# Decay attention and mixer: a new SBUF layout on the right side, pair-wise masks and token sums, operand builds and stores at other places

## The chip, the core and the metric

One NeuronCore of one Trainium2 chip runs the whole kernel. The metric is device time in microseconds (us). Three runs of the kernel before took 592.5, 596.78 and 596.5 us, median 596.5.

## The reference, cut to what matters

```python
# q, k, v: [B=4, H=8, S=768, D=64]; lam: [8], one decay per head
for b in range(nb):                       # blocks of 64 positions
    intra = einsum('bhic,bhjc->bhij', qb, kb) * Dmask     # lam ** (i - j), lower triangle
    intra = einsum('bhij,bhjd->bhid', intra, vb)
    inter = einsum('bhid,bhde->bhie', qb * lam_pow, kv_state)
    out[:, :, sl] = intra + inter
    kv_state = lam_block * kv_state + einsum('bhsd,bhse->bhde', kb * rev_pow, vb)
x = out.transpose(0, 2, 1, 3).reshape(B, S, 512)
# mixer: w_tok1 [768, 256], w_tok2 [256, 768], w_ch1 [512, 1536], w_ch2 [1536, 512], all float64
u = x + transpose(relu(transpose(x) @ w_tok1) @ w_tok2)
return u + relu(u @ w_ch1) @ w_ch2        # float32, [4, 768, 512]
```

The reference's blocks have 64 positions; the kernel computes the same recurrence in chunks of 128.

## The kernel before, in words

**Layout.** `uT[b]` holds the attention's output of batch b, and later the mixer's u, turned: 128 feature rows, 4 feature tiles, 768 positions. Every product of the mixer is made from a high and a low float32r half of each factor and takes three matmuls (high with high, low with high, high with low).

**Order.** The order in which the code is written is the order of each engine's queue. There is no scheduler that moves anything; an instruction that waits holds up all that stands behind it on its engine.

**Attention.** A loop `i` from -2 to 15 goes over 16 pairs (a batch and two heads) and works on several of them at once. For pair i+1 it makes scores (PE) and multiplies them with the decay masks (DVE, L306), scales the queries (POOL, L250), and makes the state (PE, a scan on DVE, and a copy `stb` on POOL, L284). For pair i it makes the outputs (L321, L331), copies them to `uT` (ACT, L338) and turns them back to positions (`turn_back`: PE L353, ACT L361 for `xhi`, DVE L362 for `xlo`). Groups of the token mixer are taken into the same loop (`take`): `token_hidden` (12 or 18 matmuls into `ph`, L444, then ACT and DVE write `hh` and `hl`) and `token_out` (6 matmuls into `pu`, L464, then a DVE add into `uT`, L469). Side work stands in the deque `waiting`, and `later(n)` takes n steps of it at fixed points.

**Weights.** The float64 weights arrive as pairs of 32-bit words. `narrow` turns 512 columns into float32 in five steps: one on ACT (L379) and four on DVE (L380, L383, L386, L389). `split` writes the high half on ACT (L371) and the low half on POOL (L372). The channel weights come in six groups of four pieces each, 0 and 1 for `c1`, 2 and 3 for `c2`. Seven combinations of `c1`'s blocks (A11, A12, A22, S1 to S4) are needed, since a channel product is done as a two-by-two block product with seven instead of eight multiplications; `split_c1` makes them with four sums on DVE (L512 to L515) and four splits.

**Operands.** `build(b, n)` makes the other factors of batch b from `uT[b]`: B11, B21, B22 and T1 to T4, each as a high half (ACT, L560) and a low half (L562, on POOL, or on DVE where `on_vector` names it). The temporaries behind T1 to T4 are DVE differences t1 to t4 (L552, L568).

**Hand-over.** After the loop 12 token groups of the last batch are left; between them stand parts of `build(1, 1)`. Then `p1.close()` gives the right side of SBUF (token weights, `hh`, `hl`, `x` halves) back, and the pool `cp` takes it.

**Channel mixer.** 24 units follow: for b = 0, 1 the weight groups 0 to 5, then for b = 2, 3 the groups 5 to 0. A unit has seven products `m1` to `m7` of six matmuls (L717) and four `out_pair`s of twelve matmuls (L794), each followed by a DVE add into `uT` (L809). `SLOTS` says in which order they stand; `background(n)` says after how many matmuls of unit n which side work is issued. `m3` accumulates onto the PSUM bank of `m5`, so it waits until the sum `c22` (L768) has read it; `m7` does so with the bank of `m6` (L750). Groups are written to DRAM after narrowing (`save`) and read back for b = 2, 3 (`restore`). Four `hidden_parts` results go through ACT and POOL (L728 to L730).

**Stores.** In the last units of each half `out_pair` turns its result with DVE transposes (L818) into `y` and issues eight DMAs of 48 KB (L822). The last block goes through PE transposes into `ylast` and leaves in three DMAs (`finish`, L844).

Of the kernel before, what the change touches and what calls it, by code (L numbers as in the profile page):

```python
# [22 lines left out]
def kernel(  # L23
# [264 lines left out]
    def scores(i):  # L288
        b, p = pairs[i]
        for g in range(2):  # L290
            pair = two_banks(f"sc{i}{g}", 3 * P)
            sc = [pair[:, h] for h in range(2)]
            for c in range(3):
                cs = slice((3 * g + c) * P, (3 * g + c + 1) * P)
                for h in range(2):
# [7 lines left out]
                    )  # L303
            for h in range(2):
                a = ap.tile([P, 3, P], F32, tag="a", bufs=8, name=f"a{i}{g}{h}")
                nc.vector.tensor_mul(  # L306
                    out=a,
                    in0=sc[h].rearrange("p (c i) -> p c i", i=P),
                    in1=mask[:, 2 * p + h, None, :].broadcast_to([P, 3, P]),
                )  # L310
# [141 lines left out]


# [26 lines left out]
    A11, A12, A22, S2, S3, S4, S1 = range(NW)  # L480

    def group_tiles(n, pool):
        return (
            pool.tile([P, NW, 2, P], F32R, tag="c1h", name=f"c1h{n}"),
            pool.tile([P, NW, 2, P], F32R, tag="c1l", name=f"c1l{n}"),
            pool.tile([P, JG, DM], F32R, tag="c2h", name=f"c2h{n}"),
            pool.tile([P, JG, DM], F32R, tag="c2l", name=f"c2l{n}"),
        )
# [221 lines left out]
    def prod(nm, to, a, o, start):  # L710
        g, b = nm
        c1h, c1l, _, _ = weights[g]
        uh, ul = ops[b][o]
        i = 0
        for t in range(2):
            for w, x in ((c1h, uh), (c1l, uh), (c1h, ul)):
                nc.tensor.matmul(  # L717
                    out=to, lhsT=w[:, a, t], rhs=x[:, t], start=(start and i == 0), stop=(i == 5),
# [297 lines left out]
```

## Time and profile before

| | |
|---|---|
| runs | 592.5, 596.78, 596.5 us; median 596.5 |
| profiled execution | 596.63 us, its span 594.8 us |
| ACT | 214.5 us busy, 36% |
| POOL | 237.6 us busy, 40% |
| `out_pair` adds (L809) | 94, 89.6 us in all |
| masks (L306) | 64, 31.2 us in all |

The engines' times overlap, so their sum is larger than the span. Where PE is busy nearly all the time, another engine's time shows only where PE waits for it. The rows of a trace give the start and the length of an instruction, and in brackets the idle time before it with the instruction whose end freed it. The stretches that matter are the attention loop (about 10 to 180 us), the hand-over (about 183 to 223), the first half of the units to about 370, the second half, and the end from 565.

### The profile page before, as it was taken

Reading aid. Unit: us, or ns where it says so; the run is one execution under the profiler, and the core shown is the slowest. Engines: PE = TensorE matmul, PEld = TensorE weight load, DVE = VectorE, ACT = ScalarE, POOL = GpSimd, SP = SyncE. Lnnn points to the kernel's source line nnn. Section 1 sums busy time; section 2 is a strip of 40 time slices with the busy share of each in tenths; the row PEclk is TensorE's granted clock in tenths of the full one; section 3 lists DMA queues with packets and bytes.
Section 4 is the critical chain, followed back from the end, with each engine's and each line's share of the span. In section 5 each row is a group of like instructions: output and inputs, shape, how many; then the busy total and the mean of one; then the engine's idle time right before and its main releaser. Section 6 shows DMA issues by size and latency. Waiting matters only on the chain.

```text
span 594.8 us, 10627 instructions
## 1 busy us (share of the span) xinstructions
PE 562.8 (95%) x4234; PEld 542.0 (91%) x4234; DVE 407.8 (69%) x633; ACT 214.5 (36%) x426; POOL 237.6 (40%) x205
## 2 busy tenths in 40 slices
PE   5998999799998979999999997999999999999994
PEld 4888889699998879999999997999999999999993
DVE  4797886767768788878878898974444444444472
ACT  3564433324244444344444344442222222222220
POOL 6675632455217444435344364872112222222220
PEclk9998999889999999999999999999999999999998
DMA  9999998868000227272725300464313132320057
GB/s 187 257 241 181 176 213 168 152 122 155 1 2 1 72 71 266 71 266 72 259 79 207 130 0 1 67 89 60 123 72 125 71 125 72 123 72 1 0 81 132
DMA packets 174289, 67.80 MB, mean 114 GB/s; under 512 B 163360, under 2 KB 164512, under 8 KB 174240
## 3 DMA queue, kind: packets, MB, share of 16 engines
q1 hardware_dynamic: 170896, 66.05, 44.8%
q10 hardware_dynamic: 3344, 1.09, 0.8%
q8 instruction: 33, 0.54, 0.4%
q14 instruction: 16, 0.13, 0.1%
HBM read 49.29 MB, written 17.83 MB: 113 GB/s over the span
## 4 chain that ended last, share of the span: by engine, by line
PE 76%; DVE 11%; issue 4%; ACT 3%; DMA 2%; POOL 2%; SPq 0%; ACTq 0%; POOLq 0%
PE po L794 28%; PE pc L717 8%; PE pa L717 7%; PE pb L717 7%; PE ph L444 5%; PE xT L321 4%; PE pu L464 4%; PE sc L297 4%; PE pd L717 4%; PE xT L331 2%; DMA vn<-in_v_dram 1%; DVE uT L809 1%; DVE cs L552 1%; PE xp L353 1%; PE kv L263 1%
## 5 line engine op out<-in xcount | busy, mean ns | idle before, releaser
L809 DVE TENSOR_TENSOR uT<-po,uT 128x768 f32<-128x768 f32 x94 | 89.6, 954 | 67.2 <-PE po L794 67.0
L730 POOL TENSOR_TENSOR h22l<-c,h22h 128x384 fp32r<-128x384 f32 x24 | 25.8, 1075 | 155.1 <-ACT h22h L729 143.8
L728 ACT ACTIVATE c<-c 128x384 f32<-128x384 f32 x72 | 37.8, 525 | 123.3 <-DVE c L768 90.6
L284 POOL COPY stb<-sv 64x320 f32<-64x320 f32 x32 | 26.7, 833 | 53.0 <-DVE sv L271 47.6
L321 PE MATMUL xT<-a,vn 128*64 128x128 f32 x384 | 37.5, 288 | 1.3 <-ACT uT L338 1.0
L338 ACT COPY uT<-xT 128x384 f32<-128x384 f32 x32 | 15.3, 478 | 59.6 <-PE xT L331 57.1
L730 POOL TENSOR_TENSOR h12l<-c,h12h 128x384 fp32r<-128x384 f32 x24 | 24.8, 1033 | 29.4 <-PE pa L717 20.8
L306 DVE TENSOR_TENSOR a<-sc,mask 128x384 f32<-128x384 f32 x64 | 31.2, 548 | 6.7 <-PE sc L297 6.5
L750 DVE TENSOR_TENSOR u<-pb,s 128x384 f32<-128x384 f32 x24 | 13.4, 557 | 29.7 <-PE pb L717 19.1
L756 ACT ACTIVATE h11h<-pa 128x384 fp32r<-128x384 f32 x24 | 11.7, 487 | 61.1 <-PE pa L717 61.1
L372 POOL TENSOR_TENSOR c1l<-cs,c1h 128x512 fp32r<-128x512 f32 (+1 forms) x20 | 23.3, 1177 | 25.4 <-ACT c1h L371 25.4
L331 PE MATMUL xT<-qs,stb 128*64 128x128 f32 x320 | 32.0, 278 | 0.0
L444 PE MATMUL ph<-xhi,w1h 128*128 128x256 f32 x96 | 28.2, 294 | 0.8 <-DVE uT L469 0.5
L730 POOL TENSOR_TENSOR h21l<-c,h21h 128x384 fp32r<-128x384 f32 x24 | 26.4, 1099 | 4.5 <-ACT h21h L729 3.1
L321 PEld LDWEIGHTS xT<-a,vn 128*64 128x64 f32 x384 | 23.0, 141 | 5.6 <-ACT uT L338 2.3
L297 PE MATMUL sc<-qT,kT 64*128 64x128 f32 x384 | 27.6, 293 | 0.2 <-ACT qT L235 0.2
L297 PEld LDWEIGHTS sc<-qT,kT 64*128 64x128 f32 x384 | 24.4, 200 | 3.5 <-issue 1.9
L444 PE MATMUL ph<-xhi,w1l 128*128 128x256 f32 x96 | 27.1, 282 | 0.0
L444 PE MATMUL ph<-xlo,w1h 128*128 128x256 f32 x96 | 27.1, 282 | 0.0
L464 PE MATMUL pu<-w2h,hh 128*128 128x384 f32 x64 | 24.0, 374 | 3.1 <-DVE uT L469 2.1
L250 POOL TENSOR_TENSOR qs<-qT,lamp 128x640 f32<-128x640 f32 x16 | 25.3, 1583 | 0.3
L362 DVE TENSOR_TENSOR xlo<-xp,xhi 128x384 fp32r<-128x384 f32 x32 | 17.7, 553 | 10.1 <-ACT xhi L361 9.9
(261 smaller groups left out, 1897.6 us busy)
## 6 DMA issues: line engine op xcount, KB each, us to landing
raw<-in_moe_w_ch_dram SPq DMA_DIRECT2D x20, 512.0 KB, 3.7
vn<-in_v_dram SPq DMA_DIRECT2D x16, 384.0 KB, 5.0
kn<-in_k_dram SPq DMA_DIRECT2D x30, 192.0 KB, 4.6
out_dram<-y SPq DMA_DIRECT2D x110, 48.0 KB, 1.9
qn<-in_q_dram SPq DMA_DIRECT2D x44, 96.0 KB, 3.1
dw<-c1h SPq DMA_DIRECT2D x4, 896.0 KB, 6.1
dw<-c1l SPq DMA_DIRECT2D x4, 896.0 KB, 7.9
c1hr<-dw SPq DMA_DIRECT2D x4, 896.0 KB, 4.4
```

Of the source, the lines that this page charges most:

```text
L284: nc.gpsimd.tensor_copy(out=st[r, :, h, :], in_=sv[r].rearrange("p (e c) -> p c e", c=NC - 1))
L297: nc.tensor.matmul(out=sc[h][:, c * P : (c + 1) * P], lhsT=kTs[i][r, cs], rhs=qTs[i][r, cs], start=True, stop=True,)
L306: nc.vector.tensor_mul(out=a, in0=sc[h].rearrange("p (c i) -> p c i", i=P), in1=mask[:, 2 * p + h, None, :].broadcast_to([P, 3, P]),)
L321: nc.tensor.matmul(out=xT[h * D : (h + 1) * D, cs], lhsT=vns[i][:, h, c, :], rhs=weights_of[i, g, h][:, cg, :], start=(cg == 0), stop=False,)
L331: nc.tensor.matmul(out=xT[h * D : (h + 1) * D, cs], lhsT=st[:, c - 1, h, :], rhs=qss[i][:, c - 1, :], start=False, stop=(cg == 2),)
L444: nc.tensor.matmul(out=ph, lhsT=w[:, c, fs], rhs=x[:, c], start=(i == 0), stop=(i == 3 * NC - 1))
L464: nc.tensor.matmul(out=pu, lhsT=h[:, kk, cs], rhs=w[:, kk, ss], start=(i == 0), stop=(i == 3 * NK - 1))
L717: nc.tensor.matmul(out=to, lhsT=w[:, a, t], rhs=x[:, t], start=(start and i == 0), stop=(i == 5), skip_group_check=not start,)
L728: nc.scalar.activation(src, src, AF.Relu)
L730: nc.gpsimd.tensor_sub(out=hl, in0=src, in1=hh.bitcast(F32))
L794: nc.tensor.matmul(out=to, lhsT=w[:, jj, t * P : (t + 1) * P], rhs=h, start=(i == 0), stop=(i == 3 * JG - 1))
L809: nc.vector.tensor_add(out=ub, in0=po, in1=ub)
```

## The change

- A new pool `hidp` on the right side outlives the token phase. It holds `w2h`, `w2l`, `hh0`, `hl0`, `hh1` and `hl1`. After the token phase the odd weight groups' `c1` take `w2h` and `w2l`, their `c2` take `hh1` and `hl1`, and raw pieces and the stores' `y` take `hh0` and `hl0`. A11 has tiles of its own, so a group is saved and restored by six DMAs instead of four.
- One DVE instruction of 128 x 768 masks the scores of both heads: 32 instructions instead of 64.
- Group 0: the four sums of `split_c1` go from DVE to POOL at i = 7. The narrowing and the split of piece 2 are queued at i = 9 instead of 8, B11 and B21 of `build(0, 0)` at i = 10 instead of 9.
- The last eight `token_out`s become four `token_out_pair`s, 12 matmuls into two banks and one add of 128 x 768. Pieces 0 and 1 of group 1 are fetched ahead of them; steps of narrowing and of `build(1, 1)` stand between them. T1 of that build goes to POOL; t3, T3, t4 to unit 0; T4 and B22 to unit 1. The side work of units 0 and 1 is written out anew.
- Units 10 to 12: the builds for b = 2, 3 stand at other places, with T1 to T4 of both on DVE (before: T1 and T2 of one).
- The stores of b = 0, 1 (64 DMAs, 16 transposes) go from units 11 and 12 to units 13 to 20. The units (1, 2) and (0, 2) are done before (1, 3), (0, 3): the last three `(0,2), (1,3), (0,3)` instead of `(1,3), (0,2), (0,3)`. The stores of b = 2 are spread over the last two units.

```diff
+    hidp = ctx.enter_context(tc.tile_pool(name="hidp", bufs=1, side="right"))
     p1 = ExitStack()
...
+            a = ap.tile([P, 2, 3, P], F32, tag="a", bufs=4, name=f"a{i}{g}")
+            nc.vector.tensor_mul(
+                out=a,
+                in0=pair.rearrange("p h (c i) -> p h c i", i=P),
+                in1=mask[:, 2 * p : 2 * p + 2, None, :].broadcast_to([P, 2, 3, P]),
+            )
             for h in range(2):
-                a = ap.tile([P, 3, P], F32, tag="a", bufs=8, name=f"a{i}{g}{h}")
-                nc.vector.tensor_mul(
...
+    def token_out_pair(b, sh, ct):
...
+        pu = two_banks(f"pu{b}{ct}{sh}", SB)
...
+        u = uT[b][:, ct : ct + 2, ss]
+        nc.vector.tensor_add(out=u, in0=pu, in1=u)
...
+    def group_tiles(n, odd):
+        pools = (cp, cp, hidp, hidp, hidp, hidp) if odd else (wa,) * 6
+        tags = ("a11h", "a11l", "w2h", "w2l", "hh1", "hl1") if odd else NAMES
...
-            lambda: nc.vector.tensor_add(out=a22, in0=a21, in1=a22),
+            lambda: eng.tensor_add(out=a22, in0=a21, in1=a22),
...
-            waiting.extend(split_c1(weights[0], w3[:, 0:512], w3[:, 512:1024]))
+            waiting.extend(split_c1(weights[0], w3[:, 0:512], w3[:, 512:1024], nc.gpsimd))
             load_piece(0, 3, w3[:, 2048:3072])
-        if i == 8:
+        if i == 9:
             waiting.extend(narrow_piece(w3[:, 1024:2048], w3[:, 0:512], w3[:, 512:1024]))
             waiting.append(split_c2(weights[0], 2, w3[:, 0:512]))
-        if i == 9:
+        if i == 10:
...
-    parts = build(1, 1, on_vector=("T2", "T1"))
-    order = deque(parts[x] for x in ("B11", "t1", "t2", "B21", "T2", "T1", "t3", "T3"))
-    while groups:
+    for _ in range(4):
         groups.popleft()()
...
+    fetch(1, 0)
+    fetch(1, 1)
+    steps = {}
+    parts = build(1, 1, on_vector=("T2",))
+    pa, pb = piece_steps(0), piece_steps(1)
+    order = [
+        [parts["t1"], parts["B11"], pa[0], pa[1]],
+        [parts["t2"], pa[2], parts["B21"], pa[3]],
+        [parts["T2"], pa[4], lambda: fetch(1, 2)],
+        [parts["T1"]],
+    ]
+    for n, fs in enumerate(order):
+        token_out_pair(B - 1, n // 2, 2 * (n % 2))
+        for f in fs:
+            f()
...
+    units[-3], units[-2] = units[-2], units[-3]
...
+        if n == 0:
+            c1, pb = steps["c1"], piece_steps(1)
+            add(12, pb[0], pb[1], pb[2], c1[0])
+            add(36, parts["t3"])
+            add(36, parts["T3"])
+            add(36, pb[3], pb[4], lambda: fetch(1, 3))
+            add(42, c1[1], parts["t4"])
+        if n == 1:
+            c1, pa = steps["c1"], piece_steps(2)
+            add(6, parts["T4"])
+            add(24, c1[2], c1[3], c1[4], c1[5], c1[6], pa[0])
+            add(36, parts["B22"])
+            add(36, pa[1], pa[2], c1[7])
+            add(60, pa[3], pa[4], lambda: fetch(2, 0))
...
-            bl = build(2, 0, cs_temps(), on_vector=("T2", "T1"))
+            second["a"] = bl = build(2, 0, cs_temps(), on_vector=("T1", "T2", "T3", "T4"))
...
-            bl = build(3, 1, cs_temps())
+            second["b"] = bl = build(3, 1, cs_temps(), on_vector=("T1", "T2", "T3", "T4"))
...
+        if NP1 + 1 <= n < NP1 + 9:
+            x = n - NP1 - 1
+            add(36, lambda: store(x // 4, x % 4))
+        if n >= NU - 2:
+            x = 2 * (n - NU + 2)
+            add(36, lambda: store(2, x))
+            add(84, lambda: store(2, x + 1))
```

The next fences show queues: the line of code, the operation, output and inputs with a number for each tile, the shape, and a count where rows are alike. First POOL around i = 7 to 9, before; `uT_63` holds group 0's narrowed pieces, `qs` scaled queries, `stb` states.

```order
L284 COPY stb_116<-sv_1383 64x5x64 x2
L372 TENSOR_TENSOR c1l_1037<-uT_63,c1h_1036 128x256
L372 TENSOR_TENSOR c1l_1037<-uT_63,c1h_1036 128x512
L250 TENSOR_TENSOR qs_1514<-qT_1399,lamp 128x640
L284 COPY stb_114<-sv_1539 64x5x64 x2
L372 TENSOR_TENSOR c1l_1037<-uT_63,c1h_1036 128x512 x2
L372 TENSOR_TENSOR c2l_1039<-uT_63,c2h_1038 128x512
L250 TENSOR_TENSOR qs_1669<-qT_1555,lamp 128x640
```

The same place of POOL's queue now:

```order
L286 COPY stb_119<-sv_1348 64x5x64 x2
L375 TENSOR_TENSOR a11l_1012<-uT_63,a11h_1011 128x256
L375 TENSOR_TENSOR c1l_1014<-uT_63,c1h_1013 128x512
L534 TENSOR_TENSOR uT_63<-uT_63 128x2x128
L535 TENSOR_TENSOR uT_63<-uT_63 128x2x128
L536 TENSOR_TENSOR uT_63<-uT_63 128x2x128
L537 TENSOR_TENSOR uT_63<-uT_63 128x2x128
L252 TENSOR_TENSOR qs_1475<-qT_1364,lamp 128x640
L286 COPY stb_117<-sv_1500 64x5x64 x2
L375 TENSOR_TENSOR c1l_1014<-uT_63,c1h_1013 128x512 x2
L252 TENSOR_TENSOR qs_1619<-qT_1516,lamp 128x640
L286 COPY stb_119<-sv_1644 64x5x64 x2
```

The four sums (L534 to L537) stand ahead of the scaled queries, and the split of piece 2 (`c2l`) has gone one pair of heads further back.

DVE at the hand-over, before; `uT_63` is the last batch, `pu` the token sums, `th`, `tl` the temporaries of `build(1, 1)`, `u_0` and `s_0` belong to unit 0:

```order
L552 TENSOR_TENSOR th_2463<-uT_61 128x768
L469 TENSOR_TENSOR uT_63<-pu_2465,uT_63 128x384
L552 TENSOR_TENSOR tl_2473<-uT_61,th_2463 128x768
L469 TENSOR_TENSOR uT_63<-pu_2475,uT_63 128x384
L469 TENSOR_TENSOR uT_63<-pu_2487,uT_63 128x384
L562 TENSOR_TENSOR T2l_2496<-tl_2473,T2h_2495 128x768
L469 TENSOR_TENSOR uT_63<-pu_2499,uT_63 128x384
L562 TENSOR_TENSOR T1l_2508<-th_2463,T1h_2507 128x768
L469 TENSOR_TENSOR uT_63<-pu_2511,uT_63 128x384
L552 TENSOR_TENSOR th_2463<-uT_61 128x768
```

And now, from the first pair's add to the add that `m7` of unit 0 waits for:

```order
L472 TENSOR_TENSOR uT_63<-pu_2409,uT_63 128x2x384
L574 TENSOR_TENSOR th_2423<-uT_61 128x768
L383 TENSOR_SCALAR cs<-raw_2405 128x512
L472 TENSOR_TENSOR uT_63<-pu_2431,uT_63 128x2x384
L574 TENSOR_TENSOR tl_2445<-uT_61,th_2423 128x768
L386 SCALAR_TENSOR_TENSOR cs<-raw_2405,cs 128x512
L389 TENSOR_SCALAR cs<-cs 128x512
L472 TENSOR_TENSOR uT_63<-pu_2453,uT_63 128x2x384
L584 TENSOR_TENSOR T2l_2468<-tl_2445,T2h_2467 128x768
L392 SCALAR_TENSOR_TENSOR cs<-cs 128x512
L472 TENSOR_TENSOR uT_63<-pu_2474,uT_63 128x2x384
L793 TENSOR_TENSOR u_0_2514<-pb_2507,s_0_2505 128x384
```

Eight adds have become four of twice the size, the four narrowing steps of piece 0 (L383 to L392) stand between them, and T1's and t3's instructions are gone from this place.

SP's queue at the end, before:

```order
L822 DMA out_dram<-y_6049 32x12x32 x16
L822 DMA out_dram<-y_6116 32x12x32 x16
L822 DMA out_dram<-y_6206 32x12x32 x14
L844 DMA out_dram<-ylast 128x3x128
```

And now:

```order
L871 DMA out_dram<-y_5909 32x12x32 x8
L871 DMA out_dram<-y_5994 32x12x32 x8
L871 DMA out_dram<-y_6064 32x12x32 x8
L871 DMA out_dram<-y_6149 32x12x32 x8
L871 DMA out_dram<-y_6187 32x12x32 x8
L871 DMA out_dram<-y_6212 32x12x32 x6
L891 DMA out_dram<-ylast 128x3x128
```

As many DMAs stand there as before, but each group of eight has a `y` of its own; the first four groups are now issued out of units 22 and 23, and only the last two out of the two sums behind unit 23.

More of the change, by code (lines that the diff above doesn't have):

```diff
@@ L366 @@
     w1l = tokp.tile([P, NC, FT], F32R, name="w1l")
-    w2h = tokp.tile([P, NK, S], F32R, name="w2h")
-    w2l = tokp.tile([P, NK, S], F32R, name="w2l")
+    w2h, w2l = (
+        hidp.tile([P, NK, S], F32R, tag=t, name=t) for t in ("w2h", "w2l")
+    )
     def split(hi, lo, src):
@@ L451, in token_hidden @@
         )
+    def token_out_pair(b, sh, ct):
+        hh, hl = hid[b]
+        pu = two_banks(f"pu{b}{ct}{sh}", SB)
+        ss = slice(sh * SB, (sh + 1) * SB)
+        for y in range(2):
+            cs = slice((ct + y) * P, (ct + y + 1) * P)
+            i = 0
+            for kk in range(NK):
+                for h, w in ((hh, w2h), (hl, w2h), (hh, w2l)):
+                    nc.tensor.matmul(
+                        out=pu[:, y], lhsT=h[:, kk, cs], rhs=w[:, kk, ss], start=(i == 0), stop=(i == 3 * NK - 1)
+                    )
+                    i += 1
+        u = uT[b][:, ct : ct + 2, ss]
+        nc.vector.tensor_add(out=u, in0=pu, in1=u)
     def token_out(b, sh, ct):
@@ L479 @@
     NW = 7
[L480 to L487, printed above, removed]
+    A12, A22, S2, S3, S4, S1, A11 = range(NW)
+    SHAPES = [[P, 2, P]] * 2 + [[P, NW - 1, 2, P]] * 2 + [[P, JG, DM]] * 2
+    NAMES = ("a11h", "a11l", "c1h", "c1l", "c2h", "c2l")
+    def group_tiles(n, odd):
+        pools = (cp, cp, hidp, hidp, hidp, hidp) if odd else (wa,) * 6
+        tags = ("a11h", "a11l", "w2h", "w2l", "hh1", "hl1") if odd else NAMES
+        return tuple(
+            pool.tile(x, F32R, tag=t, name=f"{t0}{n}") for pool, x, t, t0 in zip(pools, SHAPES, tags, NAMES)
         )
@@ L711, in prod @@
         g, b = nm
-        c1h, c1l, _, _ = weights[g]
+        wh, wl = weights[g][0:2] if a == A11 else (x[:, a] for x in weights[g][2:4])
         uh, ul = ops[b][o]
@@ L715, in prod @@
         for t in range(2):
-            for w, x in ((c1h, uh), (c1l, uh), (c1h, ul)):
+            for w, x in ((wh, uh), (wl, uh), (wh, ul)):
                 nc.tensor.matmul(
-                    out=to, lhsT=w[:, a, t], rhs=x[:, t], start=(start and i == 0), stop=(i == 5),
+                    out=to, lhsT=w[:, t], rhs=x[:, t], start=(start and i == 0), stop=(i == 5),
                     skip_group_check=not start,
@@ L723, in hidden_parts @@
     def hidden_parts(n, q, src):
-        pool = ch if q == "22" and n % 2 else cp
-        hh, hl = (pool.tile([P, SB], F32R, tag=f"h{q}{x}", name=f"h{q}{x}{n}") for x in "hl")
+        odd = n % 2 if q == "22" else 0
+        hh, hl = (cp.tile([P, SB], F32R, tag=f"h{q}{x}{odd}", name=f"h{q}{x}{n}") for x in "hl")
         hs[n][q] = hh, hl
@@ L941, in background @@
-        if n == NP1:
-            for when in (6, 12, 24, 36, 48):
-                add(when, later_parts.popleft())
+            second["a"] = bl = build(2, 0, cs_temps(), on_vector=("T1", "T2", "T3", "T4"))
+            add(12, bl["t1"], bl["B11"])
+            add(24, bl["t2"])
+            add(36, bl["T2"])
+            add(48, bl["t3"])
+            add(60, bl["T3"])
+            add(72, bl["T1"])
+            add(84, bl["B21"])
+        if n == NP1 - 1:
+            al = second["a"]
+            second["b"] = bl = build(3, 1, cs_temps(), on_vector=("T1", "T2", "T3", "T4"))
+            add(6, al["t4"])
+            add(12, al["T4"], al["B22"])
+            add(24, bl["t1"], bl["B11"])
+            add(36, bl["t2"])
+            add(48, bl["T2"])
+            add(72, bl["t3"], bl["T3"])
@@ L945, in background @@
             nxt = g - 1
-            add(6, lambda: restore(nxt, cp if nxt % 2 else wa, 0))
-            add(90, lambda: restore(nxt, cp if nxt % 2 else wa, 1))
+            add(6, lambda: restore(nxt, 0))
+            add(90, lambda: restore(nxt, 1))
         return deque(sorted(ev, key=lambda x: x[0]))
-    steps = {}
-    later_parts = deque()
+    second = {}
     def run(n, slots):
```

151 lines of the change are left out of this document (67 added, 84 removed).

## The prediction

> **What bounds the kernel now.** I read the page's head first, for the engine that is nearly always busy, and the head of the chain that ended last. Then came busy time by stretches, over the places that the change touches; then the rows where PE had waited; then what the engine named in them had done just before.
>
> ```profile
> span 594.8 us, 10627 instructions
> PE 562.8 (95%) x4234; PEld 542.0 (91%) x4234; DVE 407.8 (69%) x633; ACT 214.5 (36%) x426; POOL 237.6 (40%) x205
> PE 76%; DVE 11%; issue 4%; ACT 3%; DMA 2%; POOL 2%; SPq 0%; ACTq 0%; POOLq 0%
> ```
>
> PE is the bound. The change takes no matmul away, so all that there is to win is 594.8 - 562.8 = 32 us of PE's idle time and whatever the granted clock costs. The windows (start:end, length, then busy us and count of PE, PE's loads, DVE, ACT and POOL, then PE's clock, DMA share, GB/s) say where that is:
>
> ```profile
> 44.00:54.00 10.00, 8.00 (x92) 7.62 (x89) 8.89 (x14) 3.11 (x7) 5.65 (x5) 0.83 1.02 197
> 104.00:126.00 22.00, 18.70 (x192) 16.30 (x189) 16.48 (x30) 6.87 (x14) 9.58 (x9) 0.84 0.70 128
> 183.40:222.70 39.30, 33.92 (x183) 31.17 (x182) 33.33 (x46) 15.14 (x28) 21.63 (x15) 1.00 0.16 54
> 348.90:385.70 36.80, 32.84 (x181) 31.24 (x180) 33.55 (x41) 16.82 (x30) 26.38 (x17) 1.00 0.17 25
> 420.00:435.00 15.00, 15.00 (x88) 15.00 (x87) 6.87 (x10) 3.70 (x8) 2.33 (x3) 1.00 0.36 139
> ```
>
> In the second row PE is idle for 3.30 us and the clock is 0.84, which is worth 22 x 0.16 = 3.5 us more. In the third (the hand-over) it is idle for 5.38, in the fourth (units 10 to 12) for 3.96, both at full clock. At 420 PE has no gap, and DVE is free for more than half of the time. The waits themselves (start, length, idle before it and who ended it):
>
> ```profile
> 47.05 1.33 PE L263 MATMUL kv<-vn,kd 128*64 128x64 f32 x20 [2.00 <-DMA vn<-in_v_dram]
> ...
> 111.68 0.45 PE L464 MATMUL pu<-w2h,hh 128*128 128x384 f32 x1 [0.71 <-DVE hl L449]
> 114.88 0.55 PE L353 MATMUL xp<-ident,uT 128*128 128x128 f32 x3 [1.87 <-DVE xlo L362]
> 115.94 0.69 PE L464 MATMUL pu<-w2h,hh 128*128 128x384 f32 x1 [0.52 <-DVE uT L469]
> ...
> 187.13 0.44 PE L464 MATMUL pu<-w2h,hh 128*128 128x384 f32 x1 [0.40 <-DVE uT L469]
> 189.63 0.45 PE L464 MATMUL pu<-w2h,hh 128*128 128x384 f32 x1 [1.19 <-DVE uT L469]
> 206.19 0.44 PE L794 MATMUL po<-h21l,c2h 128*128 128x384 f32 x1 [0.61 <-POOL h21l L730]
> ...
> 213.31 0.44 PE L794 MATMUL po<-h12h,c2h 128*128 128x384 f32 x1 [1.41 <-DVE uT L809]
> 221.54 0.41 PE L717 MATMUL pc<-B22h,c1h 128*128 128x384 f32 x1 [1.64 <-DVE c L768]
> ...
> 365.85 0.44 PE L717 MATMUL pc<-B22h,c1h 128*128 128x384 f32 x1 [1.39 <-DVE c L768]
> ```
>
> Where one gap reached 1.87 or 2.00 us, the clock of its window fell to 0.83 or 0.84; where the longest was 1.64 or 1.39 it stayed at 1.00. So a stall here may cost its length and a slow stretch behind it: 3.5 us after the gap at 114.88, and 10 x 0.17 = 1.7 us after that at 47.05.
>
> **The stall at i = 8 (104 to 126).** What stood in front of it:
>
> ```profile
> 99.83 0.78 POOL L372 TENSOR_TENSOR c1l<-uT,c1h 128x256 fp32r<-128x256 f32 x1 [2.55 <-ACT c1h L371]
> 111.38 2.51 POOL L372 TENSOR_TENSOR c1l<-uT,c1h 128x512 fp32r<-128x512 f32 x2
> 112.69 0.67 ACT L379 ACTIVATE uT<-uT 128x512 f32<-128x512 f32 x1 [3.10 <-POOL c1l L372]
> 113.92 0.43 DVE L380 TENSOR_SCALAR uT<-uT 128x512 uint32<-128x512 uint32 x1 [2.30 <-POOL c1l L372]
> ```
>
> Piece 2 is narrowed into the words that the c1 splits still read. ACT's first step waits 3.10 us for POOL and holds `xhi` up; DVE's second waits 2.30 us and holds `xlo` and the token adds up. PE's three gaps (0.71 + 1.87 + 0.52 = 3.1) are their echo. Queued a step later, piece 2 finds those reads done. The four sums on POOL cost at most 4 x 0.78 = 3.1 us there (0.78 was POOL's 128 x 256 difference at 99.83, with 2.55 of waiting in front; below, nothing), in a window in which POOL is busy for 9.58 of 22 us. At most 3.3 + 3.5 = 6.8 comes back. I take off 0.8: i = 9 now has both its own DVE work and piece 2's, and two adds of about 0.4 may be late. **-6.0 us** (-1.5 if the clock drops for another gap, -6.8 at most).
>
> The Trainium skill ("TensorE: Matmul & The Clock Gate", Part 1) has the clock fall after at least one idle window of about 3.4 us. The trace does not bear that out as it stands: the longest gaps ahead of its two drops are 1.87 and 2.00 us. By that rule the 3.5 us of slow clock would not hang on these gaps and would stay, so that -2.5 would stand here for -6.0, and the +1.7 below would not come.
>
> **The hand-over (183 to 223).** Its price is set by two engines that do not run side by side:
>
> ```profile
> 184.58 2.03 DVE L552 TENSOR_TENSOR th<-uT 128x768 f32<-128x768 f32 x1
> 185.76 2.54 POOL L562 TENSOR_TENSOR B11l<-uT,B11h 128x768 fp32r<-128x768 f32 x1
> 187.00 2.11 DVE L552 TENSOR_TENSOR tl<-uT,th 128x768 f32<-128x768 f32 x1
> 190.07 1.55 DVE L562 TENSOR_TENSOR T2l<-tl,T2h 128x768 fp32r<-128x768 f32 x1
> 192.01 0.94 DVE L562 TENSOR_TENSOR T1l<-th,T1h 128x768 fp32r<-128x768 f32 x1
> 201.70 1.86 POOL L562 TENSOR_TENSOR T4l<-tl,T4h 128x768 fp32r<-128x768 f32 x1 [4.63 <-ACT T4h L560]
> 203.88 1.39 DVE L383 SCALAR_TENSOR_TENSOR raw<-raw 128x512 uint32<-128x512 uint32 x1
> 219.37 0.69 DVE L383 SCALAR_TENSOR_TENSOR raw<-raw 128x512 uint32<-128x512 uint32 x1
> L809 DVE TENSOR_TENSOR uT<-po,uT 128x768 f32<-128x768 f32 x94 | 89.6, 954 | 67.2 <-PE po L794 67.0
> ```
>
> A DVE difference from SBUF takes 0.94 with POOL idle (192.01) and 2.03 or 2.11 with POOL at work; POOL's take 1.86 or 2.54. One narrowing step takes 0.69 or 1.39. Adds from PSUM are hardly touched. Now: from the first pair's add to the add that m7 of unit 0 waits for DVE has four adds (4 x 0.954 = 3.8), t1, t2 and T2l (2.03 + 2.11 + 1.55 = 5.7), four narrowing steps (two near 0.43 as at 113.92, two of 0.69: 2.2) and an add near 0.55: 12.3 us, up to 2.1 more where three of the steps wait for POOL (0.7 each). PE has 54 matmuls there (36 of three pairs, 18 of m1, m6 and m2), at the 33.92 / 183 = 0.185 of the window 10.0 us, so PE waits 2.3 to 4.4. I take 3.6, since `B11l` and `B21l` run on POOL just then. Before it was 0.40 + 1.19. T1l, now POOL's at 1.86 instead of DVE's 0.94, is out of this sum, but T3, T4 and B22 stay on POOL beside it.
>
> In unit 1 the four c1 sums, the end of piece 1 and the start of piece 2 stand in front of the sum that m3 waits for: from unit 0's last sum on, 17 DVE instructions, about 11.5 us at the free lengths, and POOL's eight beside them (three builds of 1.86, three c1 splits near 1.26 as at 111.38, two `hidden_parts`) some 11 us. Half of those in DVE's way gives 17 us, against PE's work, which before took 221.54 - 202.65 less the waits of 0.61, 1.41 and 1.64, near 15 (202.65 is the start of DVE's last sum of unit 0, quoted here):
>
> ```profile
> 202.65 0.56 DVE L779 TENSOR_TENSOR c<-pc,u 128x384 f32<-128x384 f32 x1 [0.67 <-PE pc L717]
> ```
>
> So m3 waits about 2 to 2.5; I take 2.5 (0 with none in the way, 7 with all). With 0.25 left of the small waits the stretch has 3.6 + 2.5 + 0.25 = 6.35 us of idle time instead of 5.38: **+1.0 us**. A gap of 2.5 is above the 1.87 that brought the low clock: **+1.7 us**, priced by the shorter of the two slow stretches. The other end is that all but 1.3 us goes: -4.1.
>
> **Units 10 to 12 (349 to 386).** T1 to T4 on DVE (0.94 each when free) take POOL's lock out of unit 11; DVE, busy for 33.55 of 36.80 us there, gets more to do. The 1.39 at 365.85 stays, since t- and T-steps stand ahead of the same sum. Of the other 3.96 - 1.39 = 2.57 us I take about half: **-1.2 us** (-3 to +3).
>
> **The end.**
>
> ```profile
> 575.26 1.04 DVE L818 STREAM_TRANSPOSE y<-uT 128x384 f32<-128x384 f32 x2
> ...
> 565.30 26.32 SPq L822 DMA_DIRECT2D out_dram<-y  x46
> 587.52 0.40 ACTq L844 DMA_DIRECT2D out_dram<-ylast  x1
> 591.71 0.43 SPq L844 DMA_DIRECT2D out_dram<-ylast  x1
> ...
> out_dram<-ylast ACTq DMA_DIRECT2D x1, 192.0 KB, 3.0
> out_dram<-ylast SPq DMA_DIRECT2D x1, 192.0 KB, 2.1
> ```
>
> SP issues one store in 26.32 / 46 = 0.572 us, back to back, and the last `ylast` stands behind them until 591.71, though ACT's came out at 587.52. Now 24 of them go out in units 22 and 23; 22 are left from about 576.3 on (the transposes that end unit 23's work on DVE stand where those of 575.26 end): 576.3 + 22 x 0.572 = 588.9, 2.8 earlier. ACT's branch, 587.52 + 3.0 = 590.5 against 591.71 + 2.1 = 593.8, caps it at 3.3. **-2.9 us.**
>
> **What I cost at nothing.**
> ```profile
> L306 DVE TENSOR_TENSOR a<-sc,mask 128x384 f32<-128x384 f32 x64 | 31.2, 548 | 6.7 <-PE sc L297 6.5
> c1lr<-dw SPq DMA_DIRECT2D x4, 896.0 KB, 6.4
> ```
>
> Two masks cost 2 x 0.548 = 1.10, one of both heads about 0.954 (the L809 row, same shape, one PSUM input): 32 times 0.14 off an engine for which PE does not wait in those iterations. The 64 moved stores are hidden at 420, where DVE is busy for 6.87 of 15 us and DMA for 0.36; without that cover each of the 16 transposes would cost its 1.04 / 2 = 0.52, 8.3 in all. Swapping the units leaves the last restore one unit (90 matmuls, 15 us by the row of 420) for a landing of 6.4. A11's own tiles add two DMAs a group to SP's queue, whose stores and saves PE doesn't wait for; if a restore came late, it would cost up to 6.4. The wait at 47.05 and its slow clock stay: nothing near it moves.
>
> **Sum.** 596.63 - 6.0 + 1.0 + 1.7 - 1.2 - 2.9 = 589.2, so **589 us**. The profiled run is 0.13 above the median of 596.5.
>
> **The rivals.**
> *The hand-over's idle time goes.* T1l leaves DVE and the pairs halve the adds' number; if POOL's builds don't fall on DVE's: 596.6 - 6.0 - 4.1 - 1.2 - 2.9 = 582.4. The 2.03 and 2.11 speak against it, the 0.94 at 192.01 for it.
> *The stall moves to i = 9.* Piece 2's four steps stand in a fuller iteration and a gap near 1.9 takes the clock down again: -1.5 instead of -6.0: 593.7. POOL's longer queue at i = 7 speaks for it.
> *Idle windows must be longer.* If the clock falls for another reason than these gaps, the stall's slow 3.5 us stays and the hand-over's 1.7 doesn't come: 596.6 - 2.5 + 1.0 - 1.2 - 2.9 = 591.0. Against it stands that both drops follow on the two longest gaps; for it, that there are only two. It is what the page of the Trainium skill named above would give ("TensorE: Matmul & The Clock Gate").
> *Slower: DVE and POOL take turns throughout the hand-over.* DVE's 33.33 us there have some 5 of waits for POOL in them, POOL's 21.63 about 1: in full alternation 28 + 21 = 49 against PE's 33.9: 15 idle instead of 5.4, +9.6, with a slow stretch of 3.5: 596.6 - 6.0 + 9.6 + 3.5 - 1.2 - 2.9 = 599.6. It decides once the hand-over loses more than 6.0 + 1.2 + 2.9 = 10.1. The adds from PSUM that run through speak against it; every row of 2 us speaks for it.
>
> **How the numbers follow.** The forecast has 0.44 (its own range 585 to 593); the emptied hand-over 0.24; the moved stall 0.15; the other clock 0.07; the slower one 0.10. The range, **580 to 598**, leaves out half of the slower case and the edge of the 582. A measurement of this kernel tells about 1% (6 us) from no change. Below 590.5 lie two thirds of the forecast's own case (0.29), the 582 (0.24) and a little of the others (0.04): faster 0.57, same 0.38; above 602.5 half of the slower case: 0.05.
>
> **What would show it.** Right: no PE gap above 1 us and a clock near 1.0 from 104 to 126; ACT's `narrow` step of piece 2 without a wait for POOL; at the hand-over a gap before the fourth pair or m7 and one above 2 us before unit 1's m3, released by DVE; the last `ylast` at 589 or earlier; nothing new from 420 to 520. Wrong: a new gap near i = 9 with a clock below 0.9; a hand-over without gaps; PE waiting for a weight tile on a DMA, which would come from the layout, and for which I have set nothing.

## The result, and the profile after

The changed kernel takes 585.64 us (median of four runs, 585.5 to 586.22) against 596.22 of the kernel before; the ratio is 0.984 (95% interval 0.980 to 0.987). The profiled execution took 586.22 us. The page's head after (span; busy time, share and count of each engine; clock in 40 slices; chain that ended last):

```profile
span 584.4 us, 10656 instructions
PE 558.2 (96%) x4234; PEld 541.1 (93%) x4234; DVE 404.1 (69%) x598; ACT 214.5 (37%) x426; POOL 229.6 (39%) x204
PEclk9998999999999989999999999999999999999999
PE 81%; DVE 9%; DMA 3%; ACT 3%; issue 2%; POOL 1%; SPq 1%; ACTq 0%; DVEq 0%
```

PE's share of the closing chain has grown from 76% to 81%; of the two dips of the clock, one is still where it was (slice 4, near 47 us), and the other has moved (slice 15, near 215 us).

Cutting both executions at the same matmuls tells where the 10.4 us of span went. The cuts are the first score matmul of the last pair (161.0 before, 154.5 after), the first `m1` matmul of units 3, 10 and 12, and of the last unit.

| stretch | before | after | difference | forecast |
|---|---|---|---|---|
| start to the last pair's scores | 161.0 | 154.5 | -6.5 | -6.0 |
| to unit 3 (hand-over) | 77.4 | 78.8 | +1.4 | +2.7 |
| units 3 to 9 | 110.4 | 110.4 | 0.0 | 0 |
| units 10 and 11 | 36.8 | 34.6 | -2.2 | -1.2 |
| units 12 to 22 | 173.6 | 173.6 | 0.0 | 0 |
| last unit and end | 35.5 | 32.5 | -3.0 | -2.9 |

The windows of the changed kernel for the first two, the builds' units and the steady place (start:end, length; busy us and count of PE, PE's loads, DVE, ACT, POOL; clock, DMA share, GB/s):

```profile
104.00:126.00 22.00, 21.95 (x256) 20.39 (x254) 18.44 (x30) 8.17 (x18) 14.23 (x14) 1.00 0.99 176
183.00:222.00 39.00, 31.96 (x172) 31.03 (x172) 33.56 (x43) 16.28 (x30) 22.02 (x16) 0.96 0.31 114
343.70:378.30 34.60, 32.33 (x182) 31.38 (x181) 29.84 (x37) 15.93 (x29) 16.94 (x13) 1.00 0.00 0
420.00:435.00 15.00, 15.00 (x88) 15.00 (x86) 7.91 (x12) 3.99 (x8) 3.06 (x3) 1.00 0.35 93
```

The first row shows what the change bought: PE, idle for 3.3 us before and at a clock of 0.84, is busy for all of it at full clock, though DMA's share has risen from 0.70 to 0.99. The second shows a price: 7.04 us idle, 5.38 before, and 0.96. In the last, with the moved stores beside it, PE still has no gap. PE's waits behind 180 us and up to the end of unit 11 (start, length, idle before and releaser) and DVE instructions that stood in front of the first three:

```profile
184.79 0.44 PE L467 MATMUL pu<-w2h,hh 128*128 128x384 f32 x1 [1.45 <-DVE uT L472]
191.92 0.45 PE L760 MATMUL pb<-T3h,c1h 128*128 128x384 f32 x1 [1.65 <-DVE u L793]
215.08 0.66 PE L760 MATMUL pc<-B22h,c1h 128*128 128x384 f32 x1 [3.93 <-DVE c L811]
...
360.28 0.44 PE L760 MATMUL pc<-B22h,c1h 128*128 128x384 f32 x1 [1.47 <-DVE c L811]
377.17 0.44 PE L760 MATMUL pc<-B22h,c1h 128*128 128x384 f32 x1 [0.79 <-DVE c L811]
```

```profile
180.08 1.81 DVE L574 TENSOR_TENSOR th<-uT 128x768 f32<-128x768 f32 x1
181.81 2.05 DVE L383 TENSOR_SCALAR cs<-raw 128x512 uint32<-128x512 uint32 x1
...
187.33 2.60 DVE L584 TENSOR_TENSOR T2l<-tl,T2h 128x768 fp32r<-128x768 f32 x1
...
209.40 2.22 DVE L386 SCALAR_TENSOR_TENSOR cs<-raw,cs 128x512 uint32<-128x512 uint32 x1
```

The stalls stand where the forecast put them: before the fourth pair, before m7 of unit 0, before m3 of unit 1, each released by DVE. Four DVE instructions there take 8.7 us where their free lengths (0.94, 0.43, 0.94, 0.69 in the prediction's rows) make 3.0. The end, SP's queue after:

```profile
544.03 36.16 SPq L871 DMA_DIRECT2D out_dram<-y  x46
580.49 0.39 SPq L891 DMA_DIRECT2D out_dram<-ylast  x1
```

The 46 stores now start in unit 22 and end at 580.19. The `ylast` behind them goes out at 580.49, and ACT's last one, which waits for PE's last transposes, at 579.78; before they went at 591.71 and 587.52. The two branches now end nearly together.

### The profile page after: what moved, and what is told of

Its sections match the earlier page's. It is cut to its first block, busy times and chain, and to the rows that moved or that the text cites. A ratio compares the mean times of both kernels' runs of the same rounds, so it can differ in the third digit from the quotient of the medians.

```text
span 584.4 us, 10656 instructions
## 1 busy us (share of the span) xinstructions
PE 558.2 (96%) x4234; PEld 541.1 (93%) x4234; DVE 404.1 (69%) x598; ACT 214.5 (37%) x426; POOL 229.6 (39%) x204
## 4 chain that ended last, share of the span: by engine, by line
PE 81%; DVE 9%; DMA 3%; ACT 3%; issue 2%; POOL 1%; SPq 1%; ACTq 0%; DVEq 0%
PE po L835 30%; PE pc L760 8%; PE pb L760 8%; PE pa L760 7%; PE ph L447 6%; PE pu L484 4%; PE xT L323 4%; PE pd L760 4%; PE sc L299 3%; PE xT L333 3%; DMA vn<-in_v_dram 1%; DMA qn<-in_q_dram 1%; DVE uT L850 1%; PE xp L355 1%; PE kv L265 1%
## 5 line engine op out<-in xcount | busy, mean ns | idle before, releaser
L307 DVE TENSOR_TENSOR a<-sc,mask 128x768 f32<-128x768 f32 x32 | 29.1, 949 | 5.9 <-PE sc L299 5.7
L375 POOL TENSOR_TENSOR c1l<-cs,c1h 128x512 fp32r<-128x512 f32 x15 | 19.6, 1320 | 22.4 <-ACT c1h L374 22.4
L299 PE MATMUL sc<-qT,kT 64*128 64x128 f32 x384 | 26.3, 284 | 0.2 <-ACT qT L237 0.2
L835 PE MATMUL po<-h12h,c2h 128*128 128x384 f32 x64 | 21.8, 341 | 0.0
```

The source lines that it names most:

```text
L299: nc.tensor.matmul(out=sc[h][:, c * P : (c + 1) * P], lhsT=kTs[i][r, cs], rhs=qTs[i][r, cs], start=True, stop=True,)
L307: nc.vector.tensor_mul(out=a, in0=pair.rearrange("p h (c i) -> p h c i", i=P), in1=mask[:, 2 * p : 2 * p + 2, None, :].broadcast_to([P, 2, ...
L835: nc.tensor.matmul(out=to, lhsT=w[:, jj, t * P : (t + 1) * P], rhs=h, start=(i == 0), stop=(i == 3 * JG - 1))
```

## The experiments

Where an interval is given, the kernel ran several times beside the kernel before; every other time is that of a single run.

**1 and 2. Which of the two edits at i = 7 to 9 removed the stall.** Experiment 1 puts the sums back, experiment 2 the piece.

```diff
-            waiting.extend(split_c1(weights[0], w3[:, 0:512], w3[:, 512:1024], nc.gpsimd))
+            waiting.extend(split_c1(weights[0], w3[:, 0:512], w3[:, 512:1024], nc.vector))
```

> The changed kernel with one edit undone: group 0's four sums are back on DVE, piece 2 stays at i = 9. My theory (piece 2, narrowed into words that the c1 splits still read, made the stall): no PE gap above 0.5 us from 104 to 126, clock 1.00 there, 585.6 us within 0.7. Rival (the sums' time on DVE made it): gaps of 1 to 3 us there, a clock below 0.95, 588 to 592 us.

```diff
-        if i == 9:
+        if i == 8:
             waiting.extend(narrow_piece(w3[:, 1024:2048], w3[:, 0:512], w3[:, 512:1024]))
```

> The changed kernel with the other edit undone: piece 2 is queued at i = 8 again, the sums stay on POOL. My theory: the splits on POOL come behind the sums, so ACT's first narrowing step waits for POOL for 3 us or more, PE has gaps of 3 us or more from 104 to 126 with a clock near 0.84, 592 us (591 to 595). Rival (the sums on POOL were enough): 585.6 us within 0.7, no such wait.

Experiment 1 took 586.91 us, a little above what my theory allowed (585.6 within 0.7, no gap above 0.5): the clock is 1.00, but there is one gap of 0.72 us near 110.5, and the step from one pair's scores to the next, 11.1 us in the changed kernel, took 12.4 there. It took 16.4 before. Experiment 2 took 589.6 us; the stall is back, with gaps of 1.92 and 0.51 us, and that step took 14.0. ACT's first narrowing step waits for POOL again, yet the clock stays at 1.00 behind the gaps:

```profile
111.81 0.67 ACT L382 ACTIVATE uT<-uT 128x512 f32<-128x512 f32 x1 [1.73 <-POOL c1l L375]
```

In the changed kernel that step, at 118.45, waits for nothing. So it is piece 2 at i = 8 that makes the stall, as the prediction had it, and taking it to i = 9 removes it; the sums on POOL are worth another 1.3 us once it is gone. The wait was shorter than expected (1.73, not 3 or more) and the slow clock didn't come, so 589.6 stands below my 591 to 595. Why it didn't come is what experiment 3 shows.

**3. Gaps of known size, and the clock.**

```diff
+            f = cs.bitcast(F32)
+            for _ in range((7, 8, 9, 10, 11, 12, 13, 15)[x]):
+                add(60, lambda: nc.vector.tensor_add(out=f[:, 1536:1920], in0=f[:, 0:384], in1=f[:, 384:768]))
             add(36, lambda: store(x // 4, x % 4))
```

> The changed kernel with DVE instructions of no use (128 x 384 sums in a free scratch) ahead of the sum that m3 waits for, 7, 8, 9, 10, 11, 12, 13 and 15 of them in units 13 to 20, so that PE gets a gap in each unit, from about 0.9 us to about 4.9 us, in a stretch that had none. Theory A (a gap above about 1.9 us brings a stretch of half clock, one of 1.65 or less doesn't, as the two traces have it): half clock behind the last five or six gaps, none behind the first two; each drop costs 1.2 to 1.7 us: 585.6 + the gaps (near 22) + 7 to 10 = 615 to 618 us. Theory B (only a gap of about 3.4 us or more does): half clock behind two or three gaps only: 610 to 613 us.

It took 628.45 us, 42.8 more, and the eight gaps were larger than planned: 1.33, 1.95, 2.50, 3.10, 3.70, 4.32, 4.87 and 6.06 us, 27.8 in all. The first two brought no slow clock, the other six did, for 3.4 or 6.8 us each: 15.4 us lost by the clock's rows, 2.6 a drop where I had put 1.2 to 1.7. So the time lies above both forecasts. Theory B is out, since gaps of 2.50 and 3.10 us brought half clock; theory A gave the right count, but not the right rule. All slow stretches begin on one grid: at 448.07, 468.55, 489.03 and 509.51, which are multiples of 3.413 us apart. Cut on that grid, windows of this kernel read:

```profile
427.59:431.00 3.41, 2.04 (x11) 2.04 (x12) 3.17 (x6) 1.99 (x5) 0.91 (x1) 1.00 0.86 306
444.66:448.07 3.41, 0.91 (x6) 0.58 (x5) 3.27 (x8) 0.51 (x1) 0.00 (x0) 1.00 0.00 0
448.07:451.48 3.41, 3.41 (x12) 3.41 (x11) 1.34 (x2) 2.55 (x7) 2.20 (x3) 0.50 0.29 43
...
506.10:509.51 3.41, 0.69 (x4) 0.37 (x3) 3.20 (x7) 0.00 (x0) 0.00 (x0) 1.00 0.49 165
509.51:512.92 3.41, 1.80 (x6) 1.80 (x7) 2.85 (x5) 1.75 (x4) 0.67 (x1) 0.50 0.35 143
512.92:516.34 3.42, 3.42 (x12) 3.42 (x11) 0.56 (x1) 1.73 (x4) 2.35 (x3) 0.50 0.00 0
```

After a window with PE busy for 0.91 of 3.41 us the next is at 0.50; after one with 2.04, it isn't. The gap of 4.32 us lies across two windows, 0.69 and 1.80 busy, and brings two slow ones. The kernel before, on its own grid, and experiment 2 on its own:

```profile
111.94:115.35 3.41, 1.54 (x9) 1.05 (x8) 1.43 (x4) 1.95 (x4) 1.95 (x2) 1.00 0.46 101
115.35:118.76 3.41, 2.89 (x13) 2.38 (x14) 2.90 (x7) 1.10 (x2) 0.75 (x1) 0.50 0.94 183
```

```profile
113.01:116.42 3.41, 1.91 (x11) 1.43 (x12) 3.38 (x8) 1.23 (x3) 0.00 (x0) 1.00 0.68 155
```

A gap of 1.87 us fell into one window before (1.54 busy, then 0.50), one of 1.92 across two in experiment 2 (1.91 busy in the emptier one, no drop). Where the grid lies differs from run to run. So what decides at full clock is how much PE does within a window, and in these windows the border lies between 1.54 and 1.91 us of 3.41. Experiment 7 (below) narrows it: 1.56 us were enough there to keep the full clock.

```profile
208.64:212.05 3.41, 1.56 (x9) 1.23 (x7) 3.41 (x4) 0.34 (x1) 3.15 (x2) 1.00 0.17 8
212.05:215.46 3.41, 1.32 (x8) 1.35 (x9) 3.24 (x6) 1.40 (x3) 0.28 (x1) 1.00 0.88 281
```

On the other side, a window with 1.65 us at the very end of experiment 1 (577.48) was followed by 0.50. So in the traces kept here the border is near 1.55 to 1.65 us, a little under half a window, and not sharper than that.

**4. The side work ahead of m3 in unit 1.**

```diff
-            add(36, pa[1], pa[2], c1[7])
-            add(60, pa[3], pa[4], lambda: fetch(2, 0))
-            add(72, split_c2(weights[1], 2, narrowed[2]))
+            add(36, c1[7])
+            add(90, pa[1], pa[2], pa[3], pa[4], lambda: fetch(2, 0))
+            add(90, split_c2(weights[1], 2, narrowed[2]))
```

> The changed kernel with the four DVE steps of piece 2 and its split moved from places 36 and 60 of unit 1 to its end, behind m3. My theory (m3 of unit 1 waits for a sum that stands behind these steps, each of which also waits for POOL; they took 4.4 us in the trace): m3's gap of 3.93 us falls below 1 us, the clock there stays at 1.00, 581.0 us (579.5 to 583). Rival (POOL's builds hold DVE up whatever stands there, or the steps are late next in unit 2): 584.5 to 586.

581.5 us, ratio 0.977 (0.972 to 0.982). PE's wait for that sum fell from 3.93 to 1.29, not quite below the 1 us I gave:

```profile
211.43 0.41 PE L760 MATMUL pc<-B22h,c1h 128*128 128x384 f32 x1 [1.29 <-DVE c L811]
```

The clock stays at 1.00 there. The rival is out. The medians differ by 4.1 us; cut at the same matmuls, the stretch to unit 3 takes 75.05 us instead of 78.83. So the four narrowing steps ahead of one sum cost 3.8 us where they stood, 3.93 - 1.29 = 2.6 of them a wait; the slow clock behind it (3.4 us at 0.50), now gone, goes with the rest.

**5. DVE and POOL at the hand-over.**

```diff
-    parts = build(1, 1, on_vector=("T2",))
+    parts = build(1, 1, on_vector=("T2", "T1", "B11", "B21"))
```

> The changed kernel with the low halves B11l, B21l and T1l of the hand-over's build on DVE instead of POOL, which has no build left in front of m7 of unit 0. My theory (DVE's work from SBUF waits for POOL's; th took 1.81, L383 2.05, T2l 2.60 us there where 0.94, 0.41 and 0.94 are their free lengths): DVE gets three differences of 0.94 more and loses 4.2 us of waiting, so the gaps before the fourth pair and before m7 (1.45 + 1.65) shrink to 1.0 to 2.2 in all and those three lengths fall below 1.0, 1.0 and 1.3 us. Rival (DVE is simply full there, the lengths have another cause): DVE is 2.8 us later, the two gaps grow to 5 to 6 us in all, and the lengths stay. In time 584.5 against 588.5 us, each within 1.

With POOL empty the three lengths are the free ones:

```profile
180.42 0.95 DVE L574 TENSOR_TENSOR th<-uT 128x768 f32<-128x768 f32 x1
...
182.15 0.42 DVE L383 TENSOR_SCALAR cs<-raw 128x512 uint32<-128x512 uint32 x1
...
186.89 0.95 DVE L584 TENSOR_TENSOR T2l<-tl,T2h 128x768 fp32r<-128x768 f32 x1
```

The two gaps are 0 and 2.03 us, 3.10 before: DVE does 2.8 us more and is 1.1 us earlier. That POOL's instructions made DVE's longer there is shown. The run took 585.89 us, above my 584.5 by more than the 1 us I gave: up to unit 2 it won 1.6 us (38.6 instead of 40.2 from the first pair of token sums on), and unit 2 gave back 0.7, which fits that 2.2 us of the slow stretch behind m3's wait of 3.93 fell into it instead of 0.75.

**6. T1 to T4 back on POOL in units 10 to 12.**

```diff
-            second["a"] = bl = build(2, 0, cs_temps(), on_vector=("T1", "T2", "T3", "T4"))
+            second["a"] = bl = build(2, 0, cs_temps(), on_vector=("T2", "T1"))
...
-            second["b"] = bl = build(3, 1, cs_temps(), on_vector=("T1", "T2", "T3", "T4"))
+            second["b"] = bl = build(3, 1, cs_temps())
```

> The changed kernel with T3, T4 of the first and T1 to T4 of the second build of units 10 to 12 on POOL again, at the new places. My theory (six POOL differences of 1.85 us hold DVE's steps up, and m3's sum comes behind them): PE is idle in units 10 to 12 for 3.5 to 6 us instead of 2.3, 587.5 us (586.5 to 590). Rival (the new places brought the gain, DVE and POOL don't matter): 585.6 us within 0.7.

My theory fell, and the rival holds by its time alone. The run took 585.25 us, as the rival had it, but that is chance: the two units took 32.4 us instead of 34.6, so it does matter which engine makes the differences, and of the waits of 1.47 and 0.79 one of 0.42 is left:

```profile
345.10:377.50 32.40, 31.98 (x182) 31.52 (x181) 27.84 (x34) 16.29 (x30) 23.47 (x16) 1.00 0.00 1
```

Some of DVE's differences are long here too (1.69 and 2.06 us), yet DVE is busy for 27.84 us instead of 29.84. So the new places are worth 36.8 - 32.4 = 4.4 us and the move to DVE costs 2.2 of them. Not all of the 4.4 need be the builds': in the kernel before, six of the stores' transposes stood in unit 11, and they are gone from it in both versions. DVE's instructions that write `y`, before:

```profile
348.90:385.70 36.80, 3.12 (x6) 1.00 0.17 25
```

The first of them starts at 374.50, behind PE's waits of 1.39, 0.78 and 0.53 us at 365.85, 370.55 and 371.70. Cut at the next matmul of `m2`, 26.2 us into the two units before and 22.9 in this run, 3.3 of the 4.4 us are already won, and no transpose can have a part in them. The other 1.1 us may be the builds' or the transposes'; no run tells them apart, and none has the places without the new layout.

(The whole run is only 0.4 us below the changed kernel's median: in it the slow clock of the hand-over lasted 6.8 us, and the stretch to unit 3 took 80.0 us instead of 78.8.)

**7. The stores of b = 2 in the last unit.**

```diff
-        if n >= NU - 2:
-            x = 2 * (n - NU + 2)
-            add(36, lambda: store(2, x))
-            add(84, lambda: store(2, x + 1))
+        if n == NU - 1:
+            add(36, lambda: store(2, 0), lambda: store(2, 1))
+            add(84, lambda: store(2, 2))
+            add(90, lambda: store(2, 3))
```

> The changed kernel with the four stores of b = 2 all in the last unit, at places 36, 36, 84 and 90, so that 46 store DMAs stand in SP's queue from there on. My theory (SP issues one in 0.57 us and the last ylast stands behind them): SP is busy without a gap to about 584.5 instead of 580.5, the time 589 us (588 to 590). Rival (the end is set by PE and the last sums, and the stores are hidden): 585.6 us within 0.7.

590.02 us, 4.4 more, and SP is at it without a gap:

```profile
559.19 25.80 SPq L871 DMA_DIRECT2D out_dram<-y  x46
585.10 0.43 SPq L891 DMA_DIRECT2D out_dram<-ylast  x1
```

One store takes 25.80 / 46 = 0.56 us of SP's time, as before. The stores' queue set the end of the kernel before, and the earlier start is what the change won there.

**8. The masks alone.**

```diff
-            a = ap.tile([P, 2, 3, P], F32, tag="a", bufs=4, name=f"a{i}{g}")
-            nc.vector.tensor_mul(
...
             for h in range(2):
+                a = ap.tile([P, 3, P], F32, tag="a", bufs=8, name=f"a{i}{g}{h}")
+                nc.vector.tensor_mul(
...
```

> The changed kernel with 64 mask instructions of 128 x 384 instead of 32 of 128 x 768. My theory (they cost DVE 2 us more in all, in iterations in which PE does not wait for them): 585.6 us within 0.8, ratio to the kernel before as for the changed kernel within 0.002. Rival (DVE is late in the attention loop as well): 587.5 us or more.

586.48 us, ratio 0.986 (0.984 to 0.988): 0.8 us above the changed kernel, at the edge of what I gave. Where the masks stand, nothing is lost: from the scores at 102 to the last pair's, both kernels take 52.5 us. A gain of the masks' cannot be told from nothing.

**9 and 10. All that helped together, and the wait near 45 us.** Experiment 9 joins experiments 4 to 6 (T1 behind m4 of unit 0, c1's last split at place 90), issues three of b = 2's four stores in unit 22, and makes the edit of experiment 10. The stores' part, and behind it experiment 10:

```diff
+        if n == NU - 2:
+            for x, when in enumerate((36, 48, 84)):
+                add(when, lambda x=x: store(2, x))
+        if n == NU - 1:
+            add(24, lambda: store(2, 3))
```

```diff
             load_v(i + 3)
+        if i == 2:
+            load_w2()
...
-        if i == 1:
-            load_w2()
```

> The changed kernel with what the runs so far favour: B11l, B21l, T1l of the hand-over on DVE and T1 behind m4 of unit 0; the steps of piece 2 behind m3 of unit 1; in units 10 to 12 T3, T4 and the second build's T1, T2 on POOL; three of the four stores of b = 2 in unit 22; and the token weights' second load issued behind one pair's v instead of ahead of it. If the gains add: hand-over 1.2 (gaps 3.10 to below 1) + 4.1 (unit 1, as measured alone) + 2 (units 10 to 12, as measured alone) + 0.5 (end) + 2 to 3.5 (the wait for v near 45 us, and the slow stretch behind it): 585.6 - 10 to 11.5 = 575 us (573 to 578). If DVE's moved steps are only late elsewhere: gaps above 1 us in units 0 to 2, 578 to 581.

> The changed kernel with one edit: the second token weights are loaded behind the v of one pair instead of ahead of it. Theory (PE's wait of 2 us near 45 us is for a v that queues behind 1.5 MB of weights, and its gap brings half clock in some runs, which makes runs differ by 1.7 us): no gap there, no slow stretch at 47, 582.8 us (582 to 584), runs within 0.7 us of one another. Rival (the DMA queues are full in this stretch whatever the order, and another transfer is late): 585.6 us within 0.7.

Both missed. Experiment 10 took 587.61 us (ratio 0.987, 0.985 to 0.990), 2.0 more than the changed kernel, and experiment 9 580.37 (0.974, 0.973 to 0.976). The wait for v is gone, but the weights are late instead, as experiment 10's rival had it, only at a higher price. PE's new wait in experiment 10, and in ACT's queue the step that holds the copy up for which PE waits:

```profile
48.92 0.44 PE L323 MATMUL xT<-a,vn 128*64 128x128 f32 x4 [3.11 <-ACT uT L340]
```

```profile
47.84 0.66 ACT L382 ACTIVATE uT<-uT 128x512 f32<-128x512 f32 x1 [1.80 <-DMA uT<-in_moe_w_tok_dram]
48.41 0.46 ACT L340 COPY uT<-xT 128x384 f32<-128x384 f32 x1
```

A narrowing step waits for the weights, and `uT`'s copy stands behind it.

**11. Experiment 9 without that edit, T1 two products earlier, and c1's last split back at place 36.**

```diff
             add(12, pb[0], pb[1], pb[2], c1[0])
+            add(24, parts["T1"])
```

> The changed kernel with all of the run before but two things: the token weights' second load stands ahead of v again, and T1 of the hand-over's build stands behind m7 of unit 0 instead of behind m4 (c1's last split stays at place 36). If the gains add: 4.1 (unit 1) + 1 (hand-over) + 2 (units 10 to 12) + 0.5 (end): 578.0 us (577 to 579.5), at most one gap above 1 us in units 0 to 2, no slow stretch behind 180 us. If the hand-over's steps on DVE are only late elsewhere: 579.5 to 581.

576.54 us (576.15 to 577.03), ratio 0.967 (0.965 to 0.970): the fastest version here, and below the 577 to 579.5 I gave. Cut at the same matmuls, the hand-over won 6.2 us against the changed kernel (72.7 instead of 78.8) where I had added up 5.1. Against experiment 9, 2.0 us are won ahead of the last pair's scores, by the load, and 2.0 in the hand-over, by T1's place and the split's together. The hand-over's window, against 31.96 of 39 us above:

```profile
183.00:222.00 39.00, 37.05 (x207) 36.02 (x207) 34.13 (x47) 18.01 (x33) 20.46 (x15) 1.00 0.37 129
```

**12. The kernel before with the part at i = 7 to 10 alone** (the sums on POOL, piece 2 at i = 9, B11 and B21 at i = 10).

```diff
-            waiting.extend(split_c1(weights[0], w3[:, 0:512], w3[:, 512:1024]))
+            waiting.extend(split_c1(weights[0], w3[:, 0:512], w3[:, 512:1024], nc.gpsimd))
...
-        if i == 8:
+        if i == 9:
...
-        if i == 9:
+        if i == 10:
```

> The kernel before with the edits at i = 7 to 10 alone (sums on POOL, piece 2 at i = 9, B11 and B21 at i = 10). My theory (this part alone removes the stall, its three gaps of 3.1 us and the slow 6.8 us behind them): no gap above 0.5 us from 104 to 126, clock 1.00 there, 589.4 us (588.5 to 590.5), 6.5 below the kernel before. Rival (part of that gain needs the masks or the new places): 591 to 593.

589.19 us, ratio 0.989 (0.986 to 0.991), 6.8 below the 595.94 of the kernel before beside it, with this in the stall's window:

```profile
104.00:126.00 22.00, 21.95 (x256) 20.39 (x254) 18.70 (x35) 8.19 (x17) 13.57 (x13) 1.00 1.00 171
```

Nearly two thirds of the change's gain is this one part.

## Why the prediction was right

The direction and the likeliest case were right: 585.64 us lies within the range of 580 to 598 and at the low edge of that case's own 585 to 593. The forecast of 589 was 3.4 too high: the stall gave 0.5 more, the hand-over cost 1.3 less, units 10 to 12 gave 1.0 more, and the profiled execution is itself 0.6 above the median.

- **The stall at i = 8** (-6.0): -6.5 in the cut executions, -6.8 alone. Its mechanism holds (experiments 2 and 12). The 0.8 taken off for a crowded i = 9 was not needed: no gap is there.
- **The hand-over** (+1.0 idle, +1.7 clock): mechanism right, size wrong. The gaps ahead of the fourth pair and m7 were 1.45 + 1.65 = 3.10 (3.6 forecast), m3's was 3.93 (2.5 forecast), and a slow stretch of 3.4 us followed. Idle time rose by 1.7 us and a slow stretch came on top, and yet the stretch grew by 1.4 in all. A term that was missing is the eight single token sums: their 48 matmuls took 11.37 us before (183.44 to 194.81), 9.65 of them busy, and in pairs 10.05 (176.93 to 186.98), 8.60 busy, so 1.05 us less of what the windows count as busy. After each wait the next matmul starts 0.28 us later instead of 0.17, and single sums wait more often. That is about half of the 2 us between what was lost and what the stretch grew by; where the rest went is not shown.
- **Units 10 to 12** (-1.2): the size was nearer than the reason. The step that failed is "T1 to T4 on DVE take POOL's lock out of unit 11": experiment 6 shows that this part costs 2.2 us, and that the places, which I had not priced, are worth 4.4 together with the stores' leaving unit 11, at least 3.3 of them without the stores.
- **The end** (-2.9): -3.0, for the reason given (experiment 7).
- **The terms at nothing**: the moved stores, the restores and A11's tiles cost nothing between units 12 and 22 (173.6 us both times); the masks' gain is not seen (experiment 8).
- **Rivals**: the emptied hand-over did not come, nor did the one in which it loses 10 us. The moved stall did not come either. Against "idle windows must be longer" (591.0) speaks that the stall's slow stretch went with its gap, and that gaps of 2.50 and 3.10 us brought half clock in experiment 3. The new slow stretch behind the 3.93 decides nothing, as a gap of that length could bring it by either rule. The Trainium skill ("TensorE: Matmul & The Clock Gate", Part 1) calls its window of about 3.4 us free-running; experiment 3 agrees with its 3.413 us grid. Its one idle window is not what it takes here: windows with PE busy for up to 1.54 of 3.41 us (one of 1.65 at the end of experiment 1) were followed by half clock. My own bound by the length of a gap (1.64 no, 1.87 yes) was wrong as well: 1.92 and 1.95 brought none.

## What to carry to other kernels

In a queue that nobody reorders, price a side step by what stands behind it: four narrowing steps, 2.2 us long in all when nothing holds them up, cost 3.8 us ahead of one sum, and moving them behind it cost nothing that showed. A stall on the busiest engine should be read together with the clock in the window after it, since the second half of its price may come or not by where the window falls. Before moving work from a slow engine to the one that feeds the bound, try new places for it where it is: here the places, with the stores gone from unit 11, gave 4.4 us and the move took 2.2 back.
